# Two edits in the first stage of an attention-and-expert kernel: which engine copies the odd half of one tile, and a declared independence between two halves of it

## The chip, the cores and the metric

The kernel runs on one core of a Trainium2 chip. The time is the device time of one execution in microseconds, and before and after are compared by the median of several runs. The profile is one further execution, recorded by the hardware profiler; it has a time and a span (from the first to the last instruction) of its own.

## The reference

```python
def attn(q, k, v, p):                       # 8 batches, 8 heads, 576 tokens, head size 64; p has 32 landmarks
    def sm_attn(qq, kk, vv):
        s = scale * np.matmul(qq, kk.transpose(0, 1, 3, 2))
        a = softmax(s)
        return np.matmul(a, vv)
    p_packed = sm_attn(p, k, v)             # landmarks look at the tokens: 32 x 64 for each head
    return sm_attn(q, p_packed, p_packed)   # tokens look at the packed landmarks

x = attn_out as 4608 x 512                  # the 8 heads side by side
h = x @ w_in                                # 512 -> 2048
g = where(h >= 1, h, where(h <= -1, 0, (h + 1) ** 2 / 4))
out = g @ w_out                             # 2048 -> 512
```

## The kernel before

**Work of one batch.** The kernel goes through eight batches. For each it turns k and q (line 377 on TensorE for the first two batches, by DMA for the others), forms the scores of the landmarks (L431, tile `sp`), takes their exponentials on ScalarE (L437, `ex`), packs v with them (L481 and L486, tile `pk`), casts the packed landmarks to bf16 (`ppT`, four small copies through the helper at L197), and takes the reciprocals of the sums (L506, `rs`). The second attention is never multiplied out with its values. The packed landmarks are multiplied with w_in instead, which gives a matrix M of 128 x 2 x 2048 for a batch (L529, tile `mp`, method `project`), and the second attention's weights become A (scores `s` L516, exponential `eT` L556, sums `sm` L561, logarithm `ln` L565, `rc` L570 on ScalarE, and the product A at L575 on VectorE). The hidden layer is then A times M: `hidden`, 16 steps `fi` for each batch, four matmuls each into tile `h` (L649). Every step is followed by a Prelu on ScalarE (`x`, L655), a second clamp (`t`, L663 on VectorE or L665 on ScalarE) and the square (`hT`, L670 on VectorE). `output` multiplies 128 rows of hT with w_out in 16 matmuls (`o`, L723), copies the sum out (`ob`) and stores it.

**M comes in quarters.** The 2048 columns of M are four quarters f of 512 columns. A quarter's tile `mp` is 128 x 2 x 512 in f32: the index g in (0, 1) is the even or odd group of heads, and each g lies in a PSUM bank of its own. Steps fi = 4f to 4f + 3 of `hidden` need quarter f. In batch 0 each quarter is a group of its own, and the first quarter is done in two parts, `gs = [0]` and `gs = [1]`, since w_in's first quarter arrives in two transfers of 64 rows each. The copies of a quarter out of PSUM are made by `taken` (L600): for f = 0 and f = 1 of batch 0 one copy for each g, on VectorE or ScalarE.

**PSUM.** One pool of three tiles of two banks each serves s, sm, mp, h, tp, sp and pk; a new tile waits for the last reader of the one whose place it takes. A second pool of two banks serves the outputs `o` and the filler.

**What sets the order.** The class `Plan` (L25) is a planner written in Python that runs when the kernel is built. Every step is a task with a rank, the steps it depends on, the buffers it takes, and `ways`: on which engine it could run and for how long the planner reckons there. Where a task has two ways, the planner puts it on the engine on which it can begin first. It sorts all tasks by their planned start, and the instructions are emitted in that order, each engine working through its own list strictly in order. Every DMA of k, q, v, w_in, w_out is issued from GpSimd's queue (POOL) with at most eight in flight. The planner also fills TensorE's planned gaps before the first output with matmuls on zeros (`warm`, L788; L791 in the profile): a gap gives so many pieces of 512 columns, and at most one of 256.

**Waits.** Semaphores are set by the tile framework: an instruction that writes a tile waits for all earlier readers of the tile. `declare_no_dep` takes such a wait away for one pair of instructions. `copy` (L194) does so already for two copies that read parts of one tile on two engines, and keeps the copies made of a tile in `readers`.

The edits touch `project` (L520), inside `attention`, and `taken`.

Of the kernel before, what the change touches and what calls it, by code (L numbers as in the profile page):

```python
# [121 lines left out]
def kernel(  # L122
# [10 lines left out]
    nc = tc.nc  # L133
# [6 lines left out]
    NP = p.shape[2]  # L140
# [12 lines left out]
    FW = 512  # L153
# [29 lines left out]
    def wide(shape, dtype, name):  # L183
        return psW.tile(shape, dtype, tag="w", name=name)

    def new(tag, shape, dtype):
        return work.tile(shape, dtype, tag=tag, name=tag, bufs=BUFS[tag])

    plan = Plan(dict(BUFS, dma=8))
    have = {}  # L190

    readers = defaultdict(list)
# [11 lines left out]
    def either(dve, act, *pairs, parted=None):  # L204

        def emit(e):
            for to, of in pairs:
                copy(e, to(), of(), parted)
        return {"DVE": (dve[0], dve[1], emit), "ACT": (act[0], act[1], emit)}
# [5 lines left out]
    w_in_sb = const.tile([P, Q, d_ff], bf16)  # L215
# [141 lines left out]
    def attention(b, at, fine):  # L357
# [162 lines left out]
        def project(fs, gs):  # L520
            if (fs[0], gs[0]) == (0, 0):
                have["M", b] = new("M", [P, G, d_ff], bf16)
            for f in fs:
                if gs[0] == 0:
                    have["mp", b, f] = wide([P, G, FW], f32, "mp")
                for a in range(Q):
                    for g in gs:
                        r = slice(g * D, (g + 1) * D)
                        nc.tensor.matmul(have["mp", b, f][a * NP:(a + 1) * NP, g], have["ppT", b][r, g, a],  # L529
                                         w_in_sb[r, a, f * FW:(f + 1) * FW], start=True, stop=True)  # L530


        merged = b >= MERGE > 0
# [1 line left out]
        for gs in [[0], [1]] if fine else [[0, 1]]:  # L535
            needs = {id(t): t for g in gs for h in range(g, H, G) for t in ready["q", h]}

            def small(e, gs=gs):
                probs(gs)
                if merged:  # L540
                    project([0], [0, 1])

            long = 0.08 + 0.12 * len(gs) + 0.24 * merged
            t = plan.add(at["s2"] + 0.01 * gs[0], {"PE": (long, long + 0.15, small)},
                         (pp if len(gs) > 1 else [pp[gs[0]]]) + list(needs.values()) + [landed["w_in", 3]] * merged,
                         ["w", "eT"] * len(gs) + ["w", "M"] * merged, mode="s")
            s2.update({g: t for g in gs})
# [5 lines left out]
        for g in range(G):  # L553
# [24 lines left out]
            r = at["sm"] + 0.2 * g  # L578
# [21 lines left out]
        def taken(r, t, f, gs):  # L600

            res = []
            for hs in [[g] for g in gs] if b == 0 and f < MPARTS else [gs]:
                w = FW * len(hs)
                res.append(plan.add(r + 0.01 + 0.02 * hs[0], either(
                    (0.1 + w / 948, 0.15 + w / 957), (0.08 + w / 1205, 0.15 + w / 1205),
                    (lambda hs=hs: have["M", b][:, hs[0]:hs[-1] + 1, f * FW:(f + 1) * FW],
                     lambda hs=hs: have["mp", b, f][:, hs[0]:hs[-1] + 1]),
                    parted=("mp", b, f) if len(hs) == 1 else None), [t]))
            for j in range(Q):  # L610
                M_of.setdefault((b, Q * f + j), []).extend(res)
            return res
# [3 lines left out]
        if merged:  # L616
            plan.release("w", taken(at["s2"] + 0.02, s2[0], 0, [0, 1]))
        for fs in groups:

            parts = [[0], [1]] if WPARTS and (b, fs) == (0, [0]) else [[0, 1]]  # L620
            r = at["M"] + at.get("M+", 2.0) * fs[0]
            copies = defaultdict(list)
            for i, gs in enumerate(parts):
                needs = [landed["w_in", 0, g] if WPARTS and f == 0 else landed["w_in", f] for f in fs for g in gs]
                t = plan.add(r + 0.02 * i, {"PE": (0.24 * len(fs), 0.24 * len(fs) + 0.17,
                                                   lambda e, fs=fs, gs=gs: project(fs, gs))},
                             pp + needs, ["w"] * len(fs) * (i == 0) + (["M"] if (fs[0], i) == (0, 0) else []),
                             mode="s", behind=[before])
                before = t
                mms.append(t)  # L630
                for f in fs:
                    copies[f] += taken(r + 0.02 * i, t, f, gs)
            for f in fs:
                plan.release("w", copies[f])
# [192 lines left out]
```

## Time and profile before

| | us |
|---|---|
| three runs of the kernel | 246.28, 246.12, 247.0 (median 246.28) |
| the profiled execution, its own time | 246.44 |
| its span, first to last instruction | 244.7 |

So 1.74 us of the profiled execution lie outside its span, and it is 0.16 us over the median of the three.

Engines in the profile are PE (TensorE's matmuls), PEld (its weight loads, which overlap them), DVE (VectorE), ACT (ScalarE), POOL (GpSimd) and SP. A row of the timeline gives the start, the time taken, the engine, the line, the operation and the tiles `out<-in` with buffer numbers left out, a count of instructions merged into the row, and, in brackets, how long the engine sat idle before it and what ended that. A TensorE matmul of 512 columns shows some 0.38 us, since matmuls are pipelined; what one adds to a string of them is the distance between starts. A record is missing here and there: the ten fillers in front of the second projected quarter show as nine.

### The profile page before, as it was taken

How to read it: one execution, taken by the hardware profiler on the slowest of the kernel's cores; microseconds unless marked ns; L12 is line 12 of the kernel's file. 1: busy time of each engine (PE TensorE's matmuls, PEld its weight loads, DVE VectorE, ACT ScalarE, POOL GpSimd, SP SyncE). 2: the span in 40 equal slices, each digit the busy share in tenths (PEclk: the TensorE clock that was granted, in tenths of full speed). 3: DMA queues.
4: the chain of work that ended last, by engine and by line, in shares of the span. 5: the costliest groups of instructions: out<-in, count | busy, mean ns of one | idle time of the engine just before them, and what ended most of it. 6: DMA issues, size and time to landing. Idle time of an engine off the chain costs nothing.

```text
span 244.7 us, 5478 instructions
## 1 busy us (share of the span) xinstructions
PE 235.9 (96%) x2185; PEld 137.1 (56%) x2222; DVE 177.0 (72%) x301; ACT 196.8 (80%) x332; POOL 29.0 (12%) x42
## 2 busy tenths in 40 slices
PE   8999989999999999999999999999999999999993
PEld 2645646465545665566465546655565455555453
DVE  4548985579978996799899559948996877775000
ACT  3586988899969987998999799899978998876111
POOL 8452130000130030031003001100000000000000
PEclk9999999999999999999999999999999999999999
DMA  7999999999399999999999999967611111122223
GB/s 163 197 206 205 205 207 204 203 156 172 116 151 237 202 169 194 214 162 216 232 148 163 240 165 135 182 120 139 142 44 46 43 46 44 43 54 79 54 75 86
DMA packets 59194, 35.85 MB, mean 147 GB/s; under 512 B 31904, under 2 KB 54688, under 8 KB 59168
## 3 DMA queue, kind: packets, MB, share of 16 engines
q0 software_dynamic: 24256, 18.25, 50.6%
q1 hardware_dynamic: 34208, 16.69, 33.9%
q10 hardware_dynamic: 704, 0.56, 0.8%
q8 instruction: 17, 0.28, 0.5%
q14 instruction: 9, 0.07, 0.1%
HBM read 37.22 MB, written 9.44 MB: 191 GB/s over the span
## 4 chain that ended last, share of the span: by engine, by line
PE 85%; DVE 5%; DMA 4%; issue 3%; ACT 2%; POOL 1%; POOLq 0%
PE o L723 47%; PE h L649 24%; DMA q<-in_q_dram 4%; PE mp L529 3%; PE o L791 2%; DVE hT L670 2%; PE sp L431 2%; PE sm L561 2%; PE pk L476 1%; DVE t L663 1%; PE s L516 1%; PE tp L377 1%; DVE M L197 1%; ACT x L655 1%; PE pk L486 1%
## 5 line engine op out<-in xcount | busy, mean ns | idle before, releaser
L723 PE MATMUL o<-w_out_sb,hT 128*128 128x512 bf16 (+1 forms) x559 | 142.3, 373 | 2.1 <-issue 0.8
L670 DVE SCALAR_TENSOR_TENSOR hT<-t 128x576 bf16<-128x576 f32 (+1 forms) x130 | 94.0, 745 | 9.1 <-ACT t L665 7.0
L655 ACT ACTIVATE x<-h 128x576 f32<-128x576 f32 (+1 forms) x130 | 78.9, 654 | 7.4 <-PE h L649 5.7
L723 PEld LDWEIGHTS <-hT 128*128 128x128 bf16 x592 | 55.6, 98 | 49.0 <-issue 5.8
L649 PE MATMUL h<-A,M 128*128 128x288 bf16 x512 | 78.8, 286 | 0.3
L649 PEld LDWEIGHTS <-M 128*128 128x128 bf16 x512 | 49.5, 98 | 27.2 <-issue 0.7
L665 ACT ACTIVATE t<-x 128x576 f32<-128x576 f32 (+1 forms) x62 | 42.9, 694 | 1.0
L663 DVE TENSOR_SCALAR t<-x 128x576 f32<-128x576 f32 (+1 forms) x68 | 31.0, 456 | 10.5 <-ACT x L655 10.4
L197 ACT CAST M<-mp 128x1024 bf16<-128x1024 f32 (+1 forms) x20 | 19.1, 991 | 5.1 <-PE mp L529 5.0
L197 ACT COPY ob<-o 128x512 f32<-128x512 f32 (+1 forms) x19 | 11.0, 577 | 14.7 <-PE o L723 14.5
L197 DVE CAST M<-mp 128x1024 bf16<-128x1024 f32 (+1 forms) x14 | 15.5, 1108 | 4.1 <-PE mp L529 4.1
L575 DVE SCALAR_TENSOR_TENSOR A<-eT,rs,rc 128x576 bf16<-128x576 bf16 x16 | 12.5, 815 | 7.2 <-ACT rc L570 7.2
L197 DVE COPY ob<-o 128x512 f32<-128x512 f32 x18 | 12.4, 691 | 6.4 <-PE o L723 5.8
L274 POOL DMA_DIRECT2D k<-in_k_dram x8 | 6.2, 779 | 75.6 <-DMA kT<-k 51.9
L791 PE MATMUL o<-zeros 128*128 128x512 bf16 (+1 forms) x42 | 13.3, 435 | 1.4 <-DVE zeros L227 1.2
L437 ACT ACTIVATE ex<-sp 96x768 bf16<-96x768 f32 x16 | 12.2, 801 | 1.9 <-PE sp L431 1.9
L556 ACT ACTIVATE eT<-s,rs 128x576 bf16<-128x576 f32 x16 | 11.0, 740 | 1.5 <-PE s L516 1.3
L274 POOL DMA_DIRECT2D v<-in_v_dram x8 | 6.8, 849 | 43.1 <-DVE vv L463 37.0
L529 PE MATMUL mp<-w_in_sb,ppT 64*32 64x512 bf16 x256 | 10.7, 380 | 0.8 <-DVE M L197 0.8
L197 ACT CAST ppT<-pk 64x128 bf16<-64x128 f32 x22 | 5.7, 260 | 6.8 <-PE pk L486 6.5
L565 ACT ACTIVATE ln<-sm 128x576 f32<-128x576 f32 x16 | 10.2, 652 | 0.5
L570 ACT ACTIVATE rc<-ln 128x576 f32<-128x576 f32 x16 | 10.3, 682 | 0.1
(50 smaller groups left out, 115.4 us busy)
## 6 DMA issues: line engine op xcount, KB each, us to landing
v<-in_v_dram POOLq DMA_DIRECT2D x8, 576.0 KB, 11.4
out_dram<-ob SPq DMA_DIRECT2D x23, 192.0 KB, 3.1
k<-in_k_dram POOLq DMA_DIRECT2D x7, 576.0 KB, 7.8
q<-in_q_dram POOLq DMA_DIRECT2D x7, 576.0 KB, 14.6
out_dram<-ob SPq DMA_DIRECT2D x24, 128.0 KB, 2.4
w_out_sb<-in_moe_w_out_dram POOLq DMA_DIRECT2D x4, 512.0 KB, 19.8
w_in_sb<-in_moe_w_in_dram POOLq DMA_DIRECT2D x3, 512.0 KB, 13.9
out_dram<-ob SPq DMA_DIRECT2D x23, 64.0 KB, 2.2
```

The lines of the kernel that those rows point to most:

```text
L197: i = (nc.vector.tensor_copy if e == "DVE" else nc.scalar.copy)(to, of)
L274: G_.dma_start(tokens(nm, b)[:, heads(hs)], rows_of(nm, b, hs))
L437: nc.scalar.activation(have["ex", b][:, :, 64 * i:64 * i + 64], have["sp", b, i][:TP, :E * X * G], AF.Exp, scale=scale)
L529: nc.tensor.matmul(have["mp", b, f][a * NP:(a + 1) * NP, g], have["ppT", b][r, g, a], w_in_sb[r, a, f * FW:(f + 1) * FW], start=True, stop ...
L575: V.scalar_tensor_tensor(have["A", b][:, g, xs], have["eT", b, g][:, xs], rs_of[b][:, g, :1], have["rc", b, g][:, xs], ALU.mult, ALU.mult)
L649: nc.tensor.matmul(have["h", b, fi][:, hf, :HALF], have["M", b][:, g, fi * P:(fi + 1) * P], have["A", b][:, g, hf], start=(g == 0), stop=( ...
L655: nc.scalar.activation(have["x", b, fi][:, hs[0]:hs[-1] + 1], have["h", b, fi][:, hs[0]:hs[-1] + 1, :HALF], AF.Prelu, bias=-1.0, alpha=0.5)
L663: V.tensor_scalar(t, x, 1.0, 0.0, ALU.add, ALU.max)
L665: nc.scalar.activation(t, x, AF.Relu, bias=1.0)
L670: V.scalar_tensor_tensor(dst, t, 1.0, t, ALU.min, ALU.mult)
L723: nc.tensor.matmul(have["o", key][:, :w], hT[:, fi, i * P:(i + 1) * P], w_out_sb[:, fi, cols], start=(fi == 0), stop=(fi == KF - 1))
L791: nc.tensor.matmul(o[:, :w], zeros[:, :P], zeros[:, :w], start=True, stop=True)
```

## The change

The first edit, in `project`: after each matmul of the part with `gs == [1]`, the matmul is declared independent of every copy that has so far read the tile. At that point this is the even half's copy. The two halves lie in two banks.

The second edit, in `taken`: for batch 0, quarter 0, the odd half, the way "DVE" is deleted, so that the planner can place that copy on ScalarE only.

```diff
@@ project
                     for g in gs:
                         r = slice(g * D, (g + 1) * D)
-                        nc.tensor.matmul(have["mp", b, f][a * NP:(a + 1) * NP, g], have["ppT", b][r, g, a],
-                                         w_in_sb[r, a, f * FW:(f + 1) * FW], start=True, stop=True)
+                        i = nc.tensor.matmul(have["mp", b, f][a * NP:(a + 1) * NP, g], have["ppT", b][r, g, a],
+                                             w_in_sb[r, a, f * FW:(f + 1) * FW], start=True, stop=True)
+                        for _, j in readers[("mp", b, f)] if gs == [1] else []:
+                            tc.declare_no_dep(i.ins, j.ins, reason="the halves of the tile lie in banks of their own")
@@ taken
                     (lambda hs=hs: have["M", b][:, hs[0]:hs[-1] + 1, f * FW:(f + 1) * FW],
                      lambda hs=hs: have["mp", b, f][:, hs[0]:hs[-1] + 1]),
                     parted=("mp", b, f) if len(hs) == 1 else None), [t]))
+                if (b, f, hs) == (0, 0, [1]):
+
+                    del res[-1].ways["DVE"]
```

The second edit changes the planner's result, and with it the order on PE, DVE and ACT from the first quarter to the second batch's exponentials. From there to the end, and on POOL and SP throughout, the order is as before. The edits shift the lines below them: L575 becomes L577, L649 L654, L655 L660, L663 L668, L665 L670, L670 L675, L723 L728, L791 L796. The filler is 13.5 pieces between the odd half and the turning of batch 1's k, where it was 16.

TensorE at the odd half of the first quarter, before (`mp` is the projected quarter; a semaphore in brackets is what the instruction waits for, DMASW6 that of the w_in transfer, DVE_49 VectorE's):

```order
L791 MATMUL o<-zeros 128x512
L529 LDWEIGHTS ppT [waits DMASW6_49]
L529 MATMUL mp<-w_in_sb,ppT 32x512 [waits DVE_49]
L529 LDWEIGHTS ppT
L529 MATMUL mp<-w_in_sb,ppT 32x512
```

and now:

```order
L796 MATMUL o<-zeros 128x512
L529 LDWEIGHTS ppT
L529 MATMUL mp<-w_in_sb,ppT 32x512 [waits DMASW6_49]
L529 LDWEIGHTS ppT
L529 MATMUL mp<-w_in_sb,ppT 32x512
```

The wait for VectorE is gone and that for the transfer is left.

ScalarE from the last `rc` of batch 0 to the casts of batch 1's `ppT`, before (`x` and `t` are the two steps behind a hidden product; 128x288 are half products):

```order
L570 ACTIVATE rc<-ln 128x576 x2
L197 CAST M<-mp 128x512
L655 ACTIVATE x<-h 128x288 x4
L665 ACTIVATE t<-x 128x288
L655 ACTIVATE x<-h 128x576 x2
L665 ACTIVATE t<-x 128x576 x2
L655 ACTIVATE x<-h 128x576 x3
L197 COPY kT<-tp 128x4x96 x2
L665 ACTIVATE t<-x 128x576
L437 ACTIVATE ex<-sp 96x12x64 x2
L655 ACTIVATE x<-h 128x576 x3
L665 ACTIVATE t<-x 128x576
```

and now:

```order
L572 ACTIVATE rc<-ln 128x576 x2
L197 CAST M<-mp 128x512
L660 ACTIVATE x<-h 128x288 x2
L197 CAST M<-mp 128x512
L670 ACTIVATE t<-x 128x288
L660 ACTIVATE x<-h 128x288 x2
L660 ACTIVATE x<-h 128x576 x2
L670 ACTIVATE t<-x 128x576 x2
L660 ACTIVATE x<-h 128x576 x3
L197 COPY kT<-tp 128x4x96 x2
L670 ACTIVATE t<-x 128x576
L437 ACTIVATE ex<-sp 96x12x64 x2
```

The odd half's cast has come in behind `rc`, and the second quarter's cast has moved behind the first product's two halves. On TensorE the first product's four matmuls now stand ahead of the second quarter's projection, not behind it; the fifth product now stands ahead of the third quarter's projection; and a third product stands ahead of batch 1's `pk`, where two did.

VectorE ahead of its last cast of M in batch 0's stage, before:

```order
L670 SCALAR_TENSOR_TENSOR hT<-t 128x576
L506 RECIPROCAL rs<-pk 128x4
L670 SCALAR_TENSOR_TENSOR hT<-t 128x576
L663 TENSOR_SCALAR t<-x 128x576
L670 SCALAR_TENSOR_TENSOR hT<-t 128x576
L197 CAST M<-mp 128x2x512
```

and now:

```order
L675 SCALAR_TENSOR_TENSOR hT<-t 128x576
L197 CAST ppT<-pk 64x128 x2
L506 RECIPROCAL rs<-pk 128x4
L675 SCALAR_TENSOR_TENSOR hT<-t 128x576 x2
L668 TENSOR_SCALAR t<-x 128x576
L675 SCALAR_TENSOR_TENSOR hT<-t 128x576
L197 CAST M<-mp 128x2x512
```

Two of batch 1's four `ppT` casts have come over from ScalarE. The cast of M in the last row was that of batch 1's first quarter and is now that of batch 0's fourth; ScalarE has batch 1's first two quarters, where it had batch 1's second and batch 0's fourth.

## The prediction

> **What bounds the kernel now.** I read the page's busy times and its chain first, then the waits, then the stretch of the change in the timeline.
>
> ```profile
> PE 235.9 (96%) x2185; PEld 137.1 (56%) x2222; DVE 177.0 (72%) x301; ACT 196.8 (80%) x332; POOL 29.0 (12%) x42
> ...
> PE 85%; DVE 5%; DMA 4%; issue 3%; ACT 2%; POOL 1%; POOLq 0%
> ```
>
> TensorE is busy for 96% of the span and makes 85% of the chain. What the edits save elsewhere counts only if TensorE comes to its next work sooner. The row of the waits (total us, times, longest us) for the wait that the first edit names:
>
> ```profile
> PE mp L529 <- DVE M L197: 0.8, 2, 0.6
> ```
>
> Two waits, 0.8 us in all: that is all the time in the run that a projection visibly waits for a copy of M. The shorter, 0.26 us at 17.32, is the one that the edit takes away; the longer comes up at 36.37. The stretch around the first, in order of time:
>
> ```profile
> 16.57 0.69 DVE L197 CAST M<-mp 128x512 bf16<-128x512 f32 x1 [2.20 <-PE mp L529]
> 16.78 1.25 ACT L570 ACTIVATE rc<-ln 128x576 f32<-128x576 f32 x2
> 16.99 0.09 PEld L529 LDWEIGHTS <-ppT 64*32 64x32 bf16 x1 [0.42 <-DMA w_in_sb<-in_moe_w_in_dram]
> 17.32 0.40 PE L529 MATMUL mp<-w_in_sb,ppT 64*32 64x512 bf16 x4 [0.26 <-DVE M L197]
> 17.65 2.33 PE L791 MATMUL o<-zeros 128*128 128x512 bf16 x9
> 17.76 0.69 DVE L197 CAST M<-mp 128x512 bf16<-128x512 f32 x1 [0.49 <-PE mp L529]
> 18.37 1.54 DVE L575 SCALAR_TENSOR_TENSOR A<-eT,rs,rc 128x576 bf16<-128x576 bf16 x2
> ...
> 19.91 0.41 PE L529 MATMUL mp<-w_in_sb,ppT 64*32 64x512 bf16 x8
> ...
> 20.39 0.58 ACT L197 CAST M<-mp 128x512 bf16<-128x512 f32 x1 [2.37 <-PE mp L529]
> ```
> ```profile
> 20.25 2.14 PE L649 MATMUL h<-A,M 128*128 128x288 bf16 x16
> ...
> 20.95 1.32 ACT L655 ACTIVATE x<-h 128x288 f32<-128x288 f32 x4
> ```
> ```profile
> L649 PE MATMUL h<-A,M 128*128 128x288 bf16 x512 | 78.8, 286 | 0.3
> ```
>
> VectorE casts the even half (16.57), TensorE waits for that, VectorE casts the odd half and only then multiplies A; meanwhile TensorE runs filler and ScalarE is idle for 2.37 us. The first hidden product starts at 20.25.
>
> **The change, step by step.** *Odd half.* Its weights were in at 16.99 and its matmuls began at 17.32. Without the wait they begin at 17.0: 0.32 us sooner. The fillers behind follow after the same 0.33 us, at 17.32.
>
> *Filler.* Ten pieces took 17.65 to 19.91, 0.226 each. Now 8.5: 1.92 us, to 19.24. *A.* The second rc ends at 16.78 + 1.25 = 18.03, the first some 0.6 us earlier. With VectorE free at 17.27 the pair of A runs from 17.5 to 19.05 (1.54), where it ended at 19.91. *The odd cast* on ScalarE starts behind rc at 18.03 and takes 0.58, to 18.61. All three are ready by 19.24, and the second quarter's projection no longer stands ahead: the first hidden product starts at **19.24, 1.01 us sooner**. ScalarE's extra cast lies in its 2.37 us of idleness; without that cover it would cost its 0.58.
>
> *ScalarE's string.* From here each product waits for the x of a product that held its place in PSUM, so ScalarE's order decides.
>
> ```profile
> 22.13 0.47 ACT L665 ACTIVATE t<-x 128x288 f32<-128x288 f32 x1
> 22.46 1.22 ACT L655 ACTIVATE x<-h 128x576 f32<-128x576 f32 x2
> 23.52 1.29 ACT L665 ACTIVATE t<-x 128x576 f32<-128x576 f32 x2
> 24.67 1.77 ACT L655 ACTIVATE x<-h 128x576 f32<-128x576 f32 x3
> ...
> 25.44 1.19 PE L377 MATMUL tp<-ident,k 96*128 96x96 bf16 x24
> ```
>
> Starts give the cost in a string: 0.30 a half x, 0.56 the half cast (20.39 to 20.95), 0.33 the half t, 0.53 a full x, 0.575 a full t. The first half product is ready at 19.24 + 0.12 + 0.29 = 19.65 (16 matmuls in 2.14 us, each lasting 0.286, so 0.12 apart), its x starts at 19.68. Then two half x, the cast, a half t, two half x, two x, two t: 0.60 + 0.56 + 0.33 + 0.60 + 1.06 + 1.15 = 4.30. The fifth product's x starts at 23.98 and ends at 24.67; it was 24.67 to 25.36. But the seventh product now waits for it, where before only the k transposes did. So TensorE, done with its other work near 23.95, stands for 0.75 us, then does that product (0.49) and half a filler (0.11): the transposes start at 25.3, **only 0.14 sooner**. Most of the first microsecond is given back here.
>
> *To the packed landmarks.*
>
> ```profile
> 27.10 0.54 PE L431 MATMUL sp<-pT,kT 128*128 128x64 bf16 x12
> ...
> 30.42 0.94 PE L481 MATMUL pk<-ex,v 96*64 96x32 bf16 x48
> ...
> 31.78 1.08 ACT L197 CAST ppT<-pk 64x128 bf16<-64x128 f32 x4
> ...
> 33.54 0.62 PE L529 MATMUL mp<-w_in_sb,ppT 64*32 64x512 bf16 x16
> ```
>
> The same work lies between the transposes and the scores, so the scores keep the 0.14: 26.96. From there to pk it was 3.32 us; with one product more ahead of it (0.49) pk starts at 30.77, and the casts of ppT 1.36 later, at 32.13.
>
> *ppT on two engines.* ScalarE took 1.08 for four in a row. VectorE's pair in batch 0 is the row for two:
>
> ```profile
> 11.94 0.58 DVE L197 CAST ppT<-pk 64x128 bf16<-64x128 f32 x2 [1.79 <-PE pk L486]
> ...
> 34.09 1.68 PE L723 MATMUL o<-w_out_sb,hT 128*128 128x512 bf16 x7
> 35.09 1.22 DVE L197 CAST M<-mp 128x1024 bf16<-128x1024 f32 x1
> ...
> 36.37 0.41 PE L529 MATMUL mp<-w_in_sb,ppT 64*32 64x512 bf16 x8 [0.59 <-DVE M L197]
> ...
> 36.84 1.01 ACT L197 CAST M<-mp 128x1024 bf16<-128x1024 f32 x1 [1.15 <-PE mp L529]
> ```
>
> Ready at 32.7, so batch 1's projection ends (16 matmuls, 33.54 to 34.09: 0.55) at 33.3, with ten output matmuls behind it instead of seven (three moved past it): 0.22 each, to 35.5. *The second wait.* At 36.37 the fourth quarter's projection waited 0.59 us for VectorE's cast of M, late behind hT and t. It now waits for ScalarE's first cast of M, which follows the ppT pair (end 32.7), one t and one x (0.58 + 0.53) and takes 1.0, as at 36.84: done at 34.8. So the projection starts at 35.55, **0.82 sooner**. VectorE's cast behind it ends at 35.55 + 0.41 + 1.22 = 37.2, when TensorE's six outputs are done too; the next product starts there.
>
> *Two transfers and a cast give some back.*
>
> ```profile
> 16.84 0.74 POOL L290 DMA_DIRECT2D w_out_sb<-in_moe_w_out_dram  x1 [1.24 <-DMA w_in_sb<-in_moe_w_in_dram]
> ...
> 19.17 0.79 POOL L274 DMA_DIRECT2D q<-in_q_dram  x1 [1.59 <-DMA w_in_sb<-in_moe_w_in_dram]
> ```
> ```profile
> q<-in_q_dram POOLq DMA_DIRECT2D x1, 576.0 KB, 21.3
> w_out_sb<-in_moe_w_out_dram POOLq DMA_DIRECT2D x1, 512.0 KB, 21.3
> ```
> ```profile
> 38.99 0.38 PE L723 MATMUL o<-w_out_sb,hT 128*128 128x512 bf16 x1
> ...
> 41.48 1.19 PE L377 MATMUL tp<-ident,q 96*128 96x96 bf16 x24
> 42.31 1.16 ACT L197 COPY qT<-tp 128x768 bf16<-128x768 bf16 x2
> ...
> 43.68 0.44 PE L516 MATMUL s<-qT,ppT 64*32 64x288 bf16 x16
> ```
>
> w_out's third quarter lands at 16.84 + 21.3 = 38.14. TensorE needs it at 38.99 now and would at 38.2, behind two products (0.98): no wait, but that caps the lead at 0.85. q of batch 1 lands at 40.47; its transposes come 2.49 behind that output, with one more output (0.22) ahead: 40.9. ScalarE then has both large copies of qT, where it had a large and a small one (1.16): some 1.45 for two, from about 41.65 to 43.1, and the scores' second half waits for them. They end near 43.45; they ended at 43.68 + 0.44 = 44.12. **Lead 0.65.** Behind this point the order is the same on every engine, and TensorE is busy for 62.1 of the 63 us from 57 on, so the lead is kept to the end:
>
> ```profile
> 57.00:120.00 63.00, 62.12 (x613) 37.01 (x622) 55.89 (x95) 56.38 (x97) 8.39 (x10) 1.00 1.12 188
> ```
>
> *Costs not shown.* That TensorE writes one bank while VectorE reads its neighbour: fillers wrote other banks during the cast at 16.57, which took 0.69 like the one at 17.76; nothing is added. The upper bound would be that the cast is doubled, 0.69, and VectorE has 0.2 us to spare before A. A cast of 512 columns on ScalarE: 0.58, the row at 20.39; both bounds are the same row.
>
> Sum: 246.44 - 0.65 = 245.8 for the profiled execution; the median lies 0.16 lower: **245.6**.
>
> **Rivals.** (1) *The transfers come sooner, or ScalarE is quicker than I add up.* If the fifth product's x is not 0.75 us behind TensorE, and w_out lands half a microsecond earlier, the lead at the fourth quarter grows to 0.82 + 0.45 and is kept: 245.0. Against it: all parts of ScalarE's string are rows, and in the stretch from 25.2 the DMA engines carry 207 GB/s, so nothing lands sooner by itself:
>
> ```profile
> 25.20:36.40 11.20, 10.51 (x170) 6.73 (x170) 10.40 (x19) 10.21 (x20) 3.10 (x4) 1.00 1.27 207
> ```
>
> (2) *It is hidden anyway.* If w_out's and q's transfers land 0.5 us later, or the qT copies hold the scores that much longer, the lead is 0.15: 246.1. For it: the two are needed within 0.1 to 0.4 us of landing. (3) *Slower: ScalarE's string starts late.* If the first product starts only at 20.1 (A or the odd cast 0.86 us later than worked out), the fifth x ends at 25.5, the seventh product keeps the k transposes until 26.15, the 0.82 at the fourth quarter is gone, and the two large qT copies still cost their 0.2: 246.28 - 0.65 + 0.86 = 246.5. It decides from 19.9 on, where the 0.65 is used up. Against it: A has 0.2 us and the odd cast 0.6 us to spare at 19.24. (4) *TensorE's clock falls* in the new gap with 2.5 fillers fewer. [...]
>
> ```profile
> 1.19 3.17 PE L791 MATMUL o<-zeros 128*128 128x512 bf16 x7 [1.19 <-DVE zeros L227]
> ```
>
> Seven in 3.17 are 0.45 each, twice the 0.226. If the 1.66 us from 25.44 to the scores doubled: +1.7, at 247.3. The granted clock is 1.00 in the row above, whose stretch holds the 0.59 us wait. [...] (5) *The edit does not act*: excluded by the order, where the wait is gone.
>
> **Numbers.** Forecast 53%, (1) 18%, (2) 13%, (3) 8%, (4) 3%; 5% I leave for a wait that none of these names, since three engines are sorted anew from 17 to 45 us, and put it on the slow side. What a measurement of this kernel can tell from no change is about 0.5%, 1.23 us. The forecast, (2) and (3) lie inside it; two thirds of (1), 12%, go beyond it; (4) and the rest, 8%, lie beyond it on the other side. So faster 0.12, same 0.80, slower 0.08. Range 244.9 to 246.9: from 0.1 below rival (1) to 0.4 above (3), which takes in a VectorE cast made longer and half of the rest. The forecast's own range is 245.2 to 246.0.
>
> **What would show it.** The odd half's matmuls at 17.0; A done near 19.05; the first product at 19.2; a new wait of TensorE near 24 for ScalarE's x, about 0.75; transposes of k near 25.3; ppT's casts 0.55 long; no wait at the fourth quarter's projection, near 35.5; the outputs near 38.2; the span 244.0. Wrong if TensorE waits for a transfer between 34 and 44 by more than 0.3 us, or if the lead at 45 is not the lead at the end.

## The result, and the profile after

The changed kernel took 245.74 us (median of 9 runs, 245.57 to 246.01), the kernel before beside it 246.28 (9 runs, 245.94 to 247.08). The ratio is 0.9974 with a 95% interval of 0.9962 to 0.9986: 0.54 us by the medians. The forecast was 245.6, and 244.0 for the span. The page of the changed kernel begins with these lines:

```profile
span 244.0 us, 5511 instructions
...
PE 238.1 (98%) x2220; PEld 136.6 (56%) x2220; DVE 176.7 (72%) x302; ACT 197.2 (81%) x331; POOL 29.1 (12%) x42
```

The span fell from 244.7 to 244.0. PE's busy time is 2.2 us higher, in a trace that holds 35 matmul records more (2220 against 2185), so that line can't be compared. The view of the waits (total us, times, longest) of TensorE has two rows:

```profile
PE o L796 <- DVE zeros L227: 1.2, 1, 1.2
PE h L654 <- ACT x L660: 0.5, 1, 0.5
```

Both waits for VectorE's copies of M, 0.8 us, are gone. A new one has come, for an x of ScalarE. The lines of the changed kernel are some five higher: `h` is L654, `x` L660, `t` L668 and L670, `hT` L675, `o` L728, the filler L796. TensorE's row in order of time:

```profile
13.47 0.32 PE L516 MATMUL s<-qT,ppT 64*32 64x288 bf16 x8
...
16.51 0.40 PE L529 MATMUL mp<-w_in_sb,ppT 64*32 64x512 bf16 x4
...
18.68 0.65 PE L654 MATMUL h<-A,M 128*128 128x288 bf16 x4
...
24.32 0.65 PE L654 MATMUL h<-A,M 128*128 128x288 bf16 x4 [0.48 <-ACT x L660]
...
24.91 1.19 PE L377 MATMUL tp<-ident,k 96*128 96x96 bf16 x24
...
32.21 0.66 PE L529 MATMUL mp<-w_in_sb,ppT 64*32 64x512 bf16 x16
...
35.06 0.41 PE L529 MATMUL mp<-w_in_sb,ppT 64*32 64x512 bf16 x8
...
42.68 0.71 PE L516 MATMUL s<-qT,ppT 64*32 64x288 bf16 x16
...
46.31 0.62 PE L529 MATMUL mp<-w_in_sb,ppT 64*32 64x512 bf16 x16
```

The first row must be read before the others. In before's profile the first score matmuls of batch 0 began at 13.96, here at 13.47, and nothing ahead of them was changed. Two rows of before:

```profile
13.96 0.32 PE L516 MATMUL s<-qT,ppT 64*32 64x288 bf16 x8
...
47.04 0.63 PE L529 MATMUL mp<-w_in_sb,ppT 64*32 64x512 bf16 x16
```

TensorE's rows here are 0.49 us early on that account; the change can't have done that. Call this start the entry. Counted from it, the first product is 1.08 us sooner than before (18.68 against 20.25), the k transposes 0.04 (24.91 against 25.44), the fourth quarter's projection 0.82 (35.06 against 36.37), and the last row 0.24.

The even half's cast and the pair of A on VectorE, the odd half's cast on ScalarE:

```profile
16.09 0.69 DVE L197 CAST M<-mp 128x512 bf16<-128x512 f32 x1 [2.20 <-PE mp L529]
...
17.00 1.55 DVE L577 SCALAR_TENSOR_TENSOR A<-eT,rs,rc 128x576 bf16<-128x576 bf16 x2 [0.22 <-ACT rc L572]
...
17.44 0.57 ACT L197 CAST M<-mp 128x512 bf16<-128x512 f32 x1
```

and ScalarE's rows up to TensorE's new wait:

```profile
20.78 1.81 ACT L660 ACTIVATE x<-h 128x288 f32<-128x288 f32 x4
22.42 1.30 ACT L670 ACTIVATE t<-x 128x576 f32<-128x576 f32 x2
23.57 1.24 ACT L660 ACTIVATE x<-h 128x576 f32<-128x576 f32 x2
```

The odd half's cast lies in what was ScalarE's idle time and runs beside A. Later two t stand ahead of the x for which TensorE waits at 23.84. TensorE's weight loads (PEld) show two rows whose idle time is put down to a transfer:

```profile
35.06 0.11 PEld L529 LDWEIGHTS <-ppT 64*32 64x32 bf16 x8 [0.42 <-DMA w_in_sb<-in_moe_w_in_dram]
...
40.69 1.05 PEld L377 LDWEIGHTS <-q 96*128 96x128 bf16 x24 [0.49 <-DMA q<-in_q_dram]
```

The first cost TensorE nothing: w_in's fourth quarter was sent at 14.51 and landed 20.2 later, at 34.71, while the ten outputs ahead of the projection lasted until 35.06. q of batch 1 was sent at 19.05 and landed 21.6 later, at 40.65, and its transposes started at 40.69. The five outputs ahead of them start at 39.45 and take 0.215 each, to 40.53, so TensorE itself lost 0.16 us there.

### The profile page after: what moved, and what is told of

The parts are those of the page before. It is cut to its first block, busy times and chain, and to the rows that moved or that the text cites. A ratio compares the mean times of both kernels' runs of the same rounds, so it can differ in the third digit from the quotient of the medians.

```text
span 244.0 us, 5511 instructions
## 1 busy us (share of the span) xinstructions
PE 238.1 (98%) x2220; PEld 136.6 (56%) x2220; DVE 176.7 (72%) x302; ACT 197.2 (81%) x331; POOL 29.1 (12%) x42
## 4 chain that ended last, share of the span: by engine, by line
PE 86%; DVE 5%; DMA 3%; ACT 2%; POOL 1%; issue 1%; ACTq 0%; POOLq 0%
PE o L728 49%; PE h L654 23%; PE mp L529 3%; DMA q<-in_q_dram 3%; DVE hT L675 3%; PE sp L431 2%; PE pk L476 2%; PE sm L563 2%; PE o L796 2%; ACT x L660 1%; PE s L516 1%; DVE t L668 1%; PE tp L377 1%; PE pk L486 1%; POOL q L274 1%
## 5 line engine op out<-in xcount | busy, mean ns | idle before, releaser
L728 PE MATMUL o<-w_out_sb,hT 128*128 128x512 bf16 (+1 forms) x592 | 147.3, 374 | 0.1
L675 DVE SCALAR_TENSOR_TENSOR hT<-t 128x576 bf16<-128x576 f32 (+1 forms) x130 | 94.0, 744 | 9.2 <-ACT t L670 7.0
L660 ACT ACTIVATE x<-h 128x576 f32<-128x576 f32 (+1 forms) x130 | 79.2, 655 | 10.2 <-PE h L654 8.6
L728 PEld LDWEIGHTS <-hT 128*128 128x128 bf16 x592 | 55.6, 98 | 49.1 <-issue 5.6
L654 PE MATMUL h<-A,M 128*128 128x288 bf16 x512 | 79.5, 286 | 0.5 <-ACT x L660 0.5
L654 PEld LDWEIGHTS <-M 128*128 128x128 bf16 x512 | 49.3, 98 | 28.6 <-issue 1.5
L670 ACT ACTIVATE t<-x 128x576 f32<-128x576 f32 (+1 forms) x62 | 42.9, 694 | 0.9
L668 DVE TENSOR_SCALAR t<-x 128x576 f32<-128x576 f32 (+1 forms) x68 | 30.8, 454 | 10.5 <-ACT x L660 10.3
L197 ACT CAST M<-mp 128x1024 bf16<-128x1024 f32 (+1 forms) x21 | 19.6, 973 | 1.6 <-PE mp L529 1.5
L577 DVE SCALAR_TENSOR_TENSOR A<-eT,rs,rc 128x576 bf16<-128x576 bf16 x16 | 12.6, 816 | 7.4 <-ACT rc L572 7.4
L197 DVE CAST M<-mp 128x1024 bf16<-128x1024 f32 (+1 forms) x13 | 14.8, 1139 | 3.7 <-PE mp L529 3.7
L796 PE MATMUL o<-zeros 128*128 128x512 bf16 (+1 forms) x44 | 13.3, 423 | 1.2 <-DVE zeros L227 1.2
L197 ACT CAST ppT<-pk 64x128 bf16<-64x128 f32 x20 | 5.2, 261 | 6.9 <-PE pk L486 6.5
```

Source lines behind the costliest of these rows:

```text
L197: i = (nc.vector.tensor_copy if e == "DVE" else nc.scalar.copy)(to, of)
L577: V.scalar_tensor_tensor(have["A", b][:, g, xs], have["eT", b, g][:, xs], rs_of[b][:, g, :1], have["rc", b, g][:, xs], ALU.mult, ALU.mult)
L654: nc.tensor.matmul(have["h", b, fi][:, hf, :HALF], have["M", b][:, g, fi * P:(fi + 1) * P], have["A", b][:, g, hf], start=(g == 0), stop=( ...
L660: nc.scalar.activation(have["x", b, fi][:, hs[0]:hs[-1] + 1], have["h", b, fi][:, hs[0]:hs[-1] + 1, :HALF], AF.Prelu, bias=-1.0, alpha=0.5)
L668: V.tensor_scalar(t, x, 1.0, 0.0, ALU.add, ALU.max)
L670: nc.scalar.activation(t, x, AF.Relu, bias=1.0)
```

## The experiments

The theory at the start (T) was that the change gains by the end of the second wait, near 36.4, and that the first wait's gain is given back. The rival (R1) was that the whole gain is the odd half's early start, which simply lasts. The stage below is worked out from two rows of TensorE in each profile: from the entry (the first `s` of batch 0) to the projection of 16 matmuls behind the score sums of batch 1, near 46.5. The groups of runs come from several chips; each ratio is to runs of before on the same chip.

| kernel | median us | ratio to before (95%) | entry | stage, us |
|---|---|---|---|---|
| before, three profiles | 246.2 to 246.3 | | 13.96, 13.39, 13.40 | 33.08, 33.14, 33.30 |
| changed, first profile | 245.74 | 0.9974 (0.9962 to 0.9986) | 13.47 | 32.84 |
| a2_after_again | 245.78 | 0.9970 (0.9949 to 0.9992) | 13.48 | 32.72 |
| e1_nodep_only | 246.08 | 0.9987 (0.9973 to 1.0000) | 13.42 | 33.06 |
| e2_copy_only | 246.19 | 0.9994 (0.9982 to 1.0006) | 13.79 | 32.98 |
| e5_second_wait_only | 245.87 | 0.9982 (0.9969 to 0.9996) | 13.92 | 32.60 |
| e3_ppt_one_engine | 245.67 | 0.9978 (0.9964 to 0.9992) | 13.40 | 33.08 |
| e10_both_waits | 245.69 | 0.9968 (0.9945 to 0.9990) | 13.42 | 32.77 |
| e11_q_sooner | 246.62 | 1.0008 (0.9986 to 1.0031) | 13.65 | 33.92 |
| e7_scalar_string_shorter | 246.15 | 0.9985 (0.9963 to 1.0008) | 13.58 | 33.34 |
| e13_fifth_x_sooner | 245.71 | 0.9979 (0.9968 to 0.9989) | 13.31 | 32.59 |
| e14_qt_shared | 245.74 | 0.9979 (0.9971 to 0.9988) | 13.84 | 32.73 |

**The same kernels again.** Is the difference of the two first profiles the change or the entry? Two more profiles of before and one of the changed kernel, with no edit.

> The kernel before, unaltered, for a second profile: its first one began the score matmuls of the first batch at 13.96 us, seven of the nine other profiles at 13.4 to 13.8, with nothing changed ahead of them. T: an entry that is sooner by 0.3 to 0.5 us is carried to the end, since before's stage starts its q transposes 0.9 us behind the landing of their load, so the span is 244.2 to 244.4 us and the lead of the changed kernel at equal entry is 0.25 to 0.4 us in these profiles. Rival: the entry is lost in this stage (the odd half's and the fourth quarter's waits take it), and the span is 244.6 to 244.8 us whatever the entry.

> As b2_before_again, a third profile of the same kernel: span and entry move together (244.7 us less what the entry is sooner than 13.96 us, within 0.1) by T, and are unrelated by the rival.

> The changed kernel unaltered, beside the next three on one chip, since its first profile began the stage of the change 0.49 us earlier than before's (the score matmuls of the first batch at 13.47 against 13.96 us), which the change can't have caused. T: 0.4 to 0.7 us faster than before; counted from the first score matmul the odd half is 0.3 us sooner, the k transposes of the second batch are not sooner, and the q transposes of the second batch start at 40.6 us or later whatever the entry, because that load lands there. R1: what the stage gains and the entry add up, and the lead at the end is their sum.

Both profiles of before entered early. The second, in order of time:

```profile
13.39 0.32 PE L516 MATMUL s<-qT,ppT 64*32 64x288 bf16 x8
...
16.75 0.40 PE L529 MATMUL mp<-w_in_sb,ppT 64*32 64x512 bf16 x4 [0.26 <-DVE M L197]
...
35.85 0.41 PE L529 MATMUL mp<-w_in_sb,ppT 64*32 64x512 bf16 x8 [0.59 <-DVE M L197]
...
46.53 0.62 PE L529 MATMUL mp<-w_in_sb,ppT 64*32 64x512 bf16 x16
```

The waits are those of the first profile, 0.26 and 0.59. The entry came 0.57 sooner and the last row 0.51: the entry is carried to the end, as T said. The spans are 244.2 and 244.3. In the third profile 0.17 more was lost, to a copy of kT at 26.6, so span and entry moved together within 0.2, not within the 0.1 expected. Of the 0.7 us between the first two spans more than half is thus the entry. The means of the stage are 33.17 before and 32.78 changed: **0.39 us**. The two groups by medians give 0.54 and 0.44. In a2_after_again the odd half starts 0.27 sooner than in b2 from the entry, the k transposes are level, and the q transposes start at 40.58, when q landed.

**The declaration alone.**

```diff
-                        nc.tensor.matmul(have["mp", b, f]...
+                        i = nc.tensor.matmul(have["mp", b, f]...
+                        for _, j in readers[("mp", b, f)] if gs == [1] else []:
+                            tc.declare_no_dep(i.ins, j.ins, ...)
```

> The kernel before with the declaration alone: the odd half's projection no longer waits for the copy of the even half, both copies stay on VectorE, and the order on every engine is that of before. Theory T (most of the gain of the change comes from the places it gives to copies of the second batch, above all the end of the wait of 0.59 us at the fourth quarter's projection near 36.4 us; what the first wait gives is mostly given back on the way): the odd half starts some 0.3 us sooner, the second wait stays, and the kernel is 0.0 to 0.3 us faster than before, less than the 0.54 us of the change. Rival R1 (the whole gain is the early start of the odd half, and it simply lasts): 0.5 us faster, as the change itself.

It is 0.12 us faster by the medians, by the ratio anything from 0 to 0.7. In its profile the odd half starts at 16.45, 0.33 sooner than in b2 from the entry, yet the stage is only 0.11 under before's mean, less than the 0.22 by which before's three differ. Rows of PEld and of TensorE tell where it went:

```profile
24.68 1.05 PEld L377 LDWEIGHTS <-k 96*128 96x128 bf16 x24 [0.38 <-DMA k<-in_k_dram]
```
```profile
32.36 0.81 PE L725 MATMUL o<-w_out_sb,hT 128*128 128x512 bf16 x3 [0.16 <-DMA w_out_sb<-in_moe_w_out_dram]
```
```profile
35.81 0.41 PE L529 MATMUL mp<-w_in_sb,ppT 64*32 64x512 bf16 x8 [0.47 <-DVE M L197]
```

The lead over b2 is 0.26 where the last fillers start (24.20) and gone at 32.36. The k transposes came up to their transfer; the output at 26.93 uses w_out's first quarter, which was sent at 11.78 and landed 15.1 later, at 26.88; and the output at 32.36 waited for the second quarter, which landed 18.7 behind 13.64, at 32.34. The second wait stands and is 0.12 shorter. In before's order at this entry, the declaration saves 0.3 us, most of which loads take back.

**The copy alone.** The changed kernel without the declaration; every engine's order is the changed kernel's.

```diff
+                if (b, f, hs) == (0, 0, [1]):
+                    del res[-1].ways["DVE"]
```

> The changed kernel without the declaration: the odd half's copy on ScalarE and the order on every engine as in the changed kernel, but the odd half's projection again waits for the even half's copy. T: the start at 18.7 us comes 0.3 us later than in the changed kernel, the second wait is still gone, and 0.3 to 0.55 us of gain stay, since the loads at 35 and 40.7 us cap what the first 20 us can give. R1: the gain falls by the 0.3 us of the wait, to 0.2 us or less. Were the copy on ScalarE the whole of it, it would equal the changed kernel.

T missed here: hardly anything of the gain is left, 0.01 us by the medians, and a stage shorter than before's mean by 0.19. The second wait is gone in this kernel too, with its 0.59. What pays it back stands in two rows:

```profile
24.96 0.65 PE L652 MATMUL h<-A,M 128*128 128x288 bf16 x4 [0.48 <-ACT x L658]
```
```profile
43.15 0.71 PE L516 MATMUL s<-qT,ppT 64*32 64x288 bf16 x16
```

The wait for ScalarE's x costs 0.48, and the scores of batch 1 take 0.71 where before took 0.44. From here to the changed kernel the gain by medians rises from 0.01 to 0.54 and 0.44: by the times, in this order the declaration's 0.3 us does last. The intervals of the ratios overlap a little, and the stage falls by 0.14 and 0.26 to the two profiles of the changed kernel, about the 0.22 by which before's three differ, so the stage alone would not show it.

**The second wait alone.** Before with three casts of M put where the change has them; VectorE's order differs in three rows, TensorE's and ScalarE's in none.

```diff
+            if (b, f) in [(1, 0), (1, 1)]:
+                for c in res:
+                    c.ways.pop("DVE", None)
+            if (b, f) in [(0, 3)]:
+                for c in res:
+                    c.ways.pop("ACT", None)
```

> The kernel before with neither edit, but with the three casts of M that the change moved elsewhere put where the change has them: the second batch's first and second quarter on ScalarE, the first batch's fourth quarter on VectorE. The order of TensorE and of ScalarE is that of before, and three rows of VectorE differ. T: the wait of 0.59 us before the fourth quarter's projection of the first batch goes or shrinks to under 0.2 us with nothing changed before 30 us, and the kernel is 0.3 to 0.6 us faster. R1: no change, within 0.15 us of before.

TensorE's rows at that place:

```profile
34.07 1.68 PE L729 MATMUL o<-w_out_sb,hT 128*128 128x512 bf16 x7
35.73 0.41 PE L529 MATMUL mp<-w_in_sb,ppT 64*32 64x512 bf16 x8
```

The projection follows the outputs without a gap; it waited 0.59 before. The stage is 0.57 shorter and the kernel 0.33 us faster by the medians (0.1 to 0.8 by the ratio). T's number holds for this wait, and R1 is wrong that nothing but the early start counts.

**Both waits in before's order.** The declaration and the three casts together:

```diff
+                            tc.declare_no_dep(i.ins, j.ins, ...)
...
+            if (b, f) in [(1, 0), (1, 1)]:
...
+            if (b, f) in [(0, 3)]:
```

> The kernel before with the three casts of M of e5_second_wait_only and the declaration of e1_nodep_only together; every engine's order is that of e5_second_wait_only, the odd half stays on VectorE. Alone they gave 0.44 and 0.32 us by the medians and, counted from the entry, 0.49 and about 0 us in the profiles. T: the fourth quarter's projection of the first batch can't start ahead of the landing of its load near 35 us, nor the q transposes ahead of theirs near 40.6 us (41.48 in before), so together 0.5 to 0.8 us, not over 0.8, and the same as the changed kernel. Rival: no caps, 0.85 us or more where the entry is early.

By the medians it gains 0.53, like the changed kernel. The stage is 0.40 shorter, not 0.33 + 0.57 = 0.90. TensorE's waits in it:

```profile
32.21 0.81 PE L731 MATMUL o<-w_out_sb,hT 128*128 128x512 bf16 x3 [0.18 <-DMA w_out_sb<-in_moe_w_out_dram]
```
```profile
35.39 0.41 PE L529 MATMUL mp<-w_in_sb,ppT 64*32 64x512 bf16 x8 [0.19 <-DMA w_in_sb<-in_moe_w_in_dram]
```

Two transfers take 0.37 of the 0.50 that is missing; that loads would cap the sum is what T said. The odd half's copy stays on VectorE here, and ScalarE's new wait does not arise.

**ppT on one engine.** The changed kernel with batch 1's four ppT copies on ScalarE again.

```diff
+        if b == 1:
+            for c in pp:
+                del c.ways["DVE"]
```

> The changed kernel with all four copies of the second batch's ppT on ScalarE, as they were before, instead of two on ScalarE and two on VectorE. The first 30 us are as in the changed kernel. T: these copies take 1.08 us instead of 0.60, the projection of the second batch begins 0.4 to 0.5 us later, and most of the gain is lost, 0.0 to 0.25 us faster than before. R1: the gain of the first 20 us stays, 0.5 us faster.

T missed again: the ratio keeps the whole gain. ScalarE and TensorE:

```profile
31.91 1.09 ACT L197 CAST ppT<-pk 64x128 bf16<-64x128 f32 x4 [0.35 <-DVE rs L509]
```
```profile
33.39 0.74 PE L532 MATMUL mp<-w_in_sb,ppT 64*32 64x512 bf16 x16
34.06 1.47 PE L731 MATMUL o<-w_out_sb,hT 128*128 128x512 bf16 x6
35.46 0.41 PE L532 MATMUL mp<-w_in_sb,ppT 64*32 64x512 bf16 x8
```

The four take 1.09 and start 0.39 later than in the changed kernel from the entry, since they wait for VectorE's rs; batch 1's projection starts 1.25 later. But five outputs stand ahead of it instead of one, and six behind it instead of ten, and the fourth quarter's projection comes only 0.47 later. Time at the first projection is no lead unless the work ahead of it is the same. Some 0.2 us come behind 46.5, where its order differs further: from there to the end of the span it is 197.4 us here and 197.6 to 197.7 in before and the changed kernel. With 0.09 in the stage that is 0.3 us in this profile; the medians say 0.53.

**A transfer sooner.** The changed kernel with 128 KB of w_out's third load sent behind q of batch 1.

```diff
+        n = Q - (f == 2)
-        dma(("w_out", f), ..., w_out_sb[:, Q * f:Q * f + Q], ...
+        dma(("w_out", f), ..., w_out_sb[:, Q * f:Q * f + n], ...
...
+                if (nm, b) == ("q", 1):
+                    G_.dma_start(w_out_sb[:, 3 * Q - 1:3 * Q], w_out_v[:, 3 * Q - 1:3 * Q])
```

> The changed kernel with the last quarter (128 KB) of w_out's third load sent behind the second batch's q instead of ahead of it; no other engine's order changes. T: q lands some 0.6 us sooner, near 40.0 us, the wait of 0.49 us before the q transposes goes where the entry is early, and the kernel is 0.1 to 0.5 us faster than the changed kernel, 0.6 to 1.0 us faster than before. Rival (the transfer is hidden in most runs): as the changed kernel within 0.1 us.

A miss, and 0.84 us slower than the changed kernel by the medians of this group. q landed at 18.78 + 21.4 = 40.18, about 0.5 sooner, but the piece put behind it was due first:

```profile
21.28 0.69 POOL L276 DMA_DIRECT2D w_out_sb<-in_moe_w_out_dram  x1 [1.69 <-DMA w_in_sb<-in_moe_w_in_dram]
```
```profile
40.88 1.24 PE L731 MATMUL o<-w_out_sb,hT 128*128 128x512 bf16 x5 [0.92 <-DMA w_out_sb<-in_moe_w_out_dram]
```

The issue itself waited 1.69 us, the piece landed 19.6 us after it at 40.88, and the outputs ahead of q's transposes needed it at 39.96. In this order there was no slack between these two loads to trade.

**ScalarE's string shorter.** First with two t's held to VectorE, then with one t moved behind the x, which hardly stirs the order.

```diff
+            if b == 0 and fi in (2, 3):
+                del t_t.ways["ACT"]
```

> The changed kernel with the second ScalarE pass of the third and fourth product of the first batch (t) held to VectorE, so that ScalarE has two passes of 0.65 us less ahead of the fifth product's x; some rows behind it move too. T: the wait of 0.48 us near 24 us goes or moves to VectorE's products, the k transposes come 0.3 to 0.5 us sooner counted from the entry, and of this at most 0.15 us is left at the end, since the loads at 35 and 40.6 us cap the lead. R1: 0.3 to 0.5 us faster than the changed kernel to the end.

The new wait went, and the second wait came back, since the planner put batch 1's first cast of M on VectorE again, behind its hT and t:

```profile
36.25 0.41 PE L529 MATMUL mp<-w_in_sb,ppT 64*32 64x512 bf16 x8 [0.47 <-DVE M L197]
```

Other losses came with it: in this profile TensorE also waited 0.22 for w_in at 16.04 and twice for w_out, 0.5 in all and 0.3 the longer time. The stage is 0.04 over the longest of before's, and the time 0.07 less by the medians. The order changed in too many places to say what each is worth. With other t's held to VectorE, so that one moves behind the x:

```diff
+            if b == 0 and fi in (3, 4):
+                del t_t.ways["ACT"]
```

> The changed kernel with one ScalarE pass (t, 0.65 us) of the first batch moved from ahead of the fifth product's x to behind it; TensorE's order differs in one filler, VectorE's in the place of one hT. T: the wait of 0.48 us before the seventh product near 24 us goes, the k transposes start 0.3 to 0.5 us sooner counted from the entry but not ahead of their load near 24.5 us, and at the end 0 to 0.25 us of it is left, since w_in's fourth quarter lands near 34.8 and q near 40.6 us: 0.4 to 0.75 us faster than before. Rival (no caps): the whole 0.45 us is kept, 0.9 to 1.0 us faster than before.

```profile
22.25 0.73 ACT L670 ACTIVATE t<-x 128x576 f32<-128x576 f32 x1
22.82 1.24 ACT L660 ACTIVATE x<-h 128x576 f32<-128x576 f32 x2
```
```profile
24.42 1.19 PE L377 MATMUL tp<-ident,k 96*128 96x96 bf16 x24 [0.19 <-DMA k<-in_k_dram]
```

One t stands ahead of the two x, the wait for x is gone, and the k transposes, 0.33 to 0.38 sooner from the entry, wait 0.19 for their load, within what T said. q landed at 18.95 + 21.2 = 40.15 in this profile and its transposes started at 40.29, so 40.6 is no fixed floor, as T had it. The stage is 0.19 shorter than the changed kernel's mean, but the medians (0.53 against 0.54 and 0.44 for the changed kernel) show no gain over it.

**The two large copies of qT.** The changed kernel with one copy on each engine swapped back.

```diff
+            if (nm, b, i) == ("q", 1, 1):
+                del ev[0].ways["ACT"], ev[1].ways["DVE"]
```

> The changed kernel with the second batch's qT copies shared as they were before: ScalarE takes one large and one small, VectorE one small and one large, instead of both large ones on ScalarE. One copy changes places on each of the two engines, nothing else moves. Counted from the first score matmul (the entry) to the projection behind the second batch's score sums near 46.5 us, before took 33.1 to 33.3 us in three profiles and the changed kernel 32.8 and 32.7. T (the second large copy on ScalarE holds the last scores, 0.71 us for the 16 matmuls instead of 0.44): the scores take 0.44 to 0.50 us, that stage 32.4 to 32.6 us, and the kernel is 0.6 to 0.8 us faster than before. Rival (the softmax behind the scores, or q's landing, holds that place anyway): the stage stays at 32.7 to 32.9 us.

A miss. The scores took 0.78, not 0.44, and the stage is the changed kernel's. VectorE's rows tell why:

```profile
41.68 0.35 DVE L197 COPY qT<-tp 128x384 bf16<-128x384 bf16 x1
41.95 0.75 DVE L677 SCALAR_TENSOR_TENSOR hT<-t 128x576 bf16<-128x576 f32 x1
42.62 0.55 DVE L197 COPY qT<-tp 128x768 bf16<-128x768 bf16 x1
```

An hT of 0.75 stands between VectorE's two copies, as in the changed kernel; in before it stood behind both. In a2_after_again ScalarE's row is

```profile
41.30 1.50 ACT L197 COPY qT<-tp 128x768 bf16<-128x768 bf16 x2
```

The last copy ends at 43.17 here and at 42.80 there, 2.28 and 2.22 behind the start of the transposes (40.89 and 40.58). So either arrangement ends the copies at about the same time, once for the hT's place and once for ScalarE's two large copies. Whether undoing both would bring 0.44 back was not tried.

## Why the prediction was right, and where its sizes were off

The forecast of 245.6 lies 0.14 us below the measured 245.74, and the time is within its own range. The mechanism was right step by step, and most sizes too as far as the fourth quarter's projection. Its times were written in the frame of before's profile, so 0.49 us is added here to those of the changed kernel's first profile.

| step | predicted | measured + 0.49 |
|---|---|---|
| odd half's matmuls | 17.0 | 17.00 |
| pair of A ends | 19.05 | 19.04 |
| first hidden product | 19.24 | 19.17 |
| the product that waits for x | 24.70, wait 0.75 | 24.81, wait 0.48 |
| k transposes | 25.3 | 25.40 |
| ppT pair | 0.58 | 0.60 |
| fourth quarter's projection | 35.55 | 35.55 |
| next product | 37.2 | 37.32 |
| q transposes | 40.9 | 41.18 (again: 41.06) |
| scores end | 43.45 | 43.88 (again: 43.76) |

"Again" is a2_after_again with its 0.48. That the first microsecond is given back at ScalarE's string, that the second wait goes, and that behind it q's load and the qT copies take some of the lead, all came about. w_out's third quarter, the other load that the prediction named, took nothing: it was sent at 16.75 and landed 21.0 later, at 37.75, before the outputs at 37.82. The new wait was put at 0.75 and was 0.48, though the product came 0.11 later than forecast: TensorE's other work lasted until 23.84 + 0.49 = 24.33, not 23.95. A smaller wait was no gain.

**The term that was mis-sized is the lead of 0.65 at the scores.** It was 0.24 in the first profile and 0.36 in the second by before's first profile, 0.39 by the means of all stages. Three parts make up what is missing: the next product was 0.12 to 0.16 late; the way from the q transposes to the end of the scores took 2.70 (40.69 to 43.39, and 40.58 to 43.28), 0.15 more than the forecast's 2.55 (ScalarE's second large copy ended 2.22 behind the start of the transposes, as forecast with 2.20, but the scores ended 0.48 behind that copy, not 0.35); and in the first profile the q transposes were held by q's landing, 0.16. The prediction named as a sign against it a wait for a transfer of over 0.3 us between 34 and 44. PEld shows 0.49 at 40.69, but outputs filled all except 0.16.

That the forecast still came within 0.14 us is in part luck: medians put the gain at 0.54 and 0.44, profiles at 0.39, and intervals of 0.3 to 0.5 us on either side hold all of these and 0.65. The prediction had also said that some 1.23 us is the least that can be told from no change; nine runs of each kernel told 0.54, with an interval of 0.3 us on either side.

**The rivals.** That the transfers come sooner (245.0) did not happen. The rival that the gain is hidden (246.1, a lead of 0.15, if the loads land 0.5 us later) came closest to what the profiles show: q landed at 40.65 + 0.49 = 41.14, 0.67 behind the forecast's 40.47, since it was sent only 0.12 sooner than in before, not 0.49, and took 21.6 instead of 21.3. The lead of 0.24 to 0.39 lies between that rival and the forecast; the median lies 0.36 under that rival's. That ScalarE's string starts late (246.5) did not: the odd cast ended at 18.01, before the pair of A at 18.55. TensorE's granted clock was 1.00 and 0.998 in the changed kernel's two profiles, with gaps of 0.48 and 0.47 us in front of the seventh product, and the stretch from the k transposes to the scores, 1.66 in before, took 1.52 (24.91 to 26.43) and 1.51 (24.97 to 26.48), not twice as long: with that the rival of 247.3 fell. The fillers of 0.45 each at 1.19, from which it was sized, ran at a granted clock of 1.00 as well (before, from 1.19 to 4.36), so that row shows slow matmuls and no fall of the clock. That VectorE's even cast would be slowed by TensorE's writing into the neighbouring bank was bounded at 0.69 us and priced at nothing: the cast took 0.69, as before, though TensorE's matmuls ran beside only its last 0.27 (16.51 to 16.78). Two engines that read two banks at once did not slow each other either: before's two casts at 20.39, one on each engine, took 0.58 and 0.69, as long as one alone (0.57 in the changed kernel at 17.44, 0.69 at 16.57). For TensorE writing beside VectorE the 0.69 above shows no slowing.

**What each edit brings.** The copy on ScalarE removes the second wait (worth 0.57 of the stage by itself in before's order) and brings a wait for x (0.48) and scores that take 0.27 longer; alone it changes the time by too little for these runs to tell. With the declaration added, the gain by medians is 0.44 to 0.54, so in that order the declaration's early start makes up the gain. In before's order the declaration alone brings nothing that stands out of the spread. So T, which gave most of the gain to the second wait, fell; R1 fits the changed kernel's order, and is wrong that nothing but the early start counts. Open: how much of e13's 0.19 in the profile is real, why e3 gains again behind 46.5, and how the stage's gain divides between the two edits, since the copy alone has one profile.

## What to carry to other kernels

Before two profiles are compared, compare a row ahead of the edit: here 0.49 of a difference of 0.73 us was there before the edit could act. A copy moved to an idle engine is costed by what its new engine does later, and by how the planner sorts everything behind it, not by the idle time it fills (here the odd half's cast lay in idle time, and an x behind it on ScalarE held TensorE for 0.48 us); hold the order fixed and move one thing to tell these apart. A lead is worth what the next load leaves of it (in e1_nodep_only it was 0.26 us at 24.20 and gone at 32.36): list the landings against the needs before adding up waits saved.

## What the hardware showed that was not expected

The entry, with the same instructions ahead of it, lay between 13.31 and 13.96 us in fourteen profiles, and before's profiles carried it to the end within 0.2. The runs of before scatter by about as much again (245.77 to 246.81 for 34 of the 35 runs beside the first group of experiments); only profiles show an entry, so whether that scatter is the entry's stays open. Nor did loads of the same size, sent at nearly the same time, land alike. w_in's fourth quarter took 20.2 us from its issue at 14.51 in the changed kernel and 21.0 from 14.53 in e1_nodep_only; in e10_both_waits 20.9 lay between its issue at 14.47 and the projection at 35.39, and TensorE waited 0.19 for it. An edit worth 0.3 us is inside that, and the intervals of e1, e2, e7 and e11 reach or include no change.
